# A bank of scores that one engine kept is kept half by ScalarE and half by VectorE: a gated attention mix on one core

## The chip, the cores and the metric

The kernel runs on one core of one Trainium2 chip. The metric is the device time of one execution in microseconds (us). Engines: TensorE (PE; its weight loads are PEld), VectorE (DVE), ScalarE (ACT), GpSimd (POOL) and SyncE (SP, which here issues the DMAs).

## The reference

Two attentions over the same x (2048 tokens, 448 features, 16 heads of 28) are mixed by a gate per token. A is linear attention with a learned feature map, B is full softmax attention; the change lies in B.

```python
x = A_x
g = _sigmoid((x * gate_w).sum(-1, keepdims=True))
a = _A_ref(x, A_wqkv, A_w_phi, A_wo)      # phi = softmax(p), softmax(-p) of a per-head linear map
b = _B_ref(x, B_wqkv, B_wo)
return g * a + (1 - g) * b
# _B_ref, per head:
scores = jnp.einsum("bhqd,bhkd->bhqk", q, k) * scale
p = _softmax(scores, axis=-1)
o = jnp.einsum("bhqk,bhkd->bhqd", p, v)   # then heads joined, @ wo
```

## The kernel before

Softmax needs the maximum of each query's scores over all 2048 keys before the exponentials. The kernel computes q.k twice. One pass finds the maxima: `mx_unit` does it in the first part of the run, and from about 339 us to 890 us `mx_visit` does it, beside the attention of earlier queries. The other pass (`scores`) computes the scores transposed, keys on the partitions, with the negated maximum already inside as one more row of the operands, so that ScalarE only has to take the exponential.

The main loop runs over steps s: 4 groups of 4 heads, 4 blocks of 512 queries, 16 blocks of 128 keys, so 256 steps. While maxima are left to find, a step consists of these, in this order:

- `scores(s)`: four matmuls st (L873), one for each head, each into its own bank of PSUM; ScalarE takes the exponential of each bank (L895) into p.
- `values(s - 1)`: p of the step before times v (L1004), added up in the bank pv. Each of its four matmuls shows as two.
- `mx_visit()`: the maxima for 128 queries of 4 heads against a block of 512 keys. This is the part that the change touches.

Each step with its visit is called a visit below. A block of keys has the number kb, 0 to 3. In a visit four matmuls pm (L322) go into four banks, one for each head, on different rows of the array. To halve the reductions for three of four heads, the keys kept for head j in block j are differences (`kd`, L196): max(a, b) = b + max(a - b, 0). So the bank of head kb is not reduced at once. It is read out to SBUF, through Relu where kb < 3, into the tile `rl` (L326, the kept tile; three buffers); one visit later VectorE adds it to the next bank of that head and takes the maximum of the sum (L330, two instructions: one over 512 columns, and one that reads the result). The other banks get a plain maximum each (L333). So VectorE's queue has, for kb = 1, 2, 3, two plain maxima and one sum with maximum; for kb = 0 it has three plain maxima and then the postponed maximum of the kept tile of kb = 3 (L336).

Banks of PSUM are handed out by a list, `free`, of seven; the eighth holds pv. A visit takes four. The bank that is read into `rl` is put back on the list at once, as the last one:

```python
def mx_banks(f, first):
    b = [free.pop(0) for _ in range(4)]
    free.append(b[0])
    held.extend(b[1:])
```

The next `scores` then finds four banks free: three that the exponentials have left, and fourth this one. So the fourth st matmul of a step goes into the bank that `rl` is read from in the visit before it. The other three banks of the visit come back after that `scores`, and the next visits and scores take them.

The order on each engine is written out by hand (a manual schedule); every engine takes its own queue in order. The waits between engines are put in when the program is built, from what each instruction reads and writes. At the end of a group of 16 steps VectorE copies pv out (L399), before the visit of that step; a reciprocal (L409) and a small reduction with a transposition for the maxima (L250, L255) follow in later steps.

Of the kernel before, what the change touches and what calls it, by code (L numbers as in the profile page):

```python
# [11 lines left out]
AF = mybir.ActivationFunctionType  # L12
# [28 lines left out]
def gated_mix_kernel(ctx, tc, xT, wqkB, wvB, wvA, wkAT, wqAT, phi, woA, woB,  # L41
# [7 lines left out]
    nc = tc.nc  # L49
# [136 lines left out]
    def mx_load(g, c):  # L186
        mxs[("kc", g, c)] = r = mx_tile("kc", f"kc{g}_{c}", 5)
        if c == 0:
            mxs["kd"] = mx_tile("kd", f"kd{g}", 1)
            for h in range(3):  # L190
                mx_rows(mxs["kd"], (h,), k_d[g], (h,), h * 512)
        for h in range(4):
            mx_rows(r, (h,), k_d[g], (h,), 512 * (c + (c == h and c < 3) - (c == h + 1 and c > 0)))
        if c < 3:
            js, t = slice(32 * c, 32 * c + DH), mxs["kd"]
            diffs.append((mxs["u"] + mxs["f"] // 4, lambda: nc.gpsimd.tensor_sub(  # L196
                r[js], f32(r[js]), f32(t[js]))))

    def take_diffs(n):
        while diffs and diffs[0][0] + n <= mxs["u"] + mxs["f"] // 4:  # L200
            diffs.pop(0)[1]()

    def mx_query(gq):
        g, qb = divmod(gq, NQ)
        mxs[("qc", gq)] = mx_rows(mx_tile("qc", f"qc{gq}", 3), range(4), q_d[g], range(4), qb * 512)
# [32 lines left out]
    def mx_reduce(gq):  # L238

        col = 64 * gq  # L240
        if gq < GM:
            parts = [(0, 4, col, 2)]
        elif gq == GM:
            parts = [(0, QM, col, 2), (QM, 4, col + 8 * QM, 4)]
        else:
            parts = [(0, 4, col, 4)]

        def reduce():
            for a, z, c, n in parts:
                nc.vector.tensor_reduce(  # L250
                    red[:, :16].rearrange("p (h t) -> p h t", t=4)[:, :, a:z],
                    part[:, c:c + 4 * (z - a) * n].rearrange("p (k t h) -> p h t k", t=z - a, h=4),
                    AX.X, ALU.max)
            nm_of[gq] = nm = mxp.tile([P, 32], F32, tag="nm", name=f"nm{gq}", bufs=7)
            nc.vector.transpose(nm, f32(red))  # L255

        mxs["fin"].append(reduce)
# [47 lines left out]
    def mx_visit():  # L305


        take_diffs(2)
        f = mxs["f"]
        todo = flats[f:f + 4]  # L310
        fins = mxs["fin"][:1 if todo and todo[0][1] == 0 else None]
        del mxs["fin"][:len(fins)]
        mxs["f"] = f + len(todo)
        if todo:
            gq, kb, qt, _, col = todo[0]
            g, qb = divmod(gq, NQ)
            if kb == 1 and qt in (0, QM) and gq + 1 < NG * NQ and ("qc", gq + 1) not in mxs:
                mx_query(gq + 1)
            pm = mx_banks(f, kb)
            for j in sorted(range(4), key=lambda j: j != kb):  # L320
                js = slice(32 * j, 32 * j + DH)
                nc.tensor.matmul(pm[j], mxs[("qc", gq)][js, qt * P:(qt + 1) * P],  # L322
                                 mxs[("kc", g, kb)][js, :], start=True, stop=True,
                                 tile_position=(32 * j, 0))
            rl = late_p.tile([P, 512], F32, tag="rl", name=f"rl{f}", bufs=3)
            nc.scalar.activation(rl, pm[kb], AF.Relu if kb < 3 else AF.Copy)  # L326
            for j in sorted({0, 1, 2, 3} - {kb}, key=lambda j: j == kb - 1):
                if j == kb - 1:
                    r = mxs["rl"]
                    nc.vector.tensor_tensor_reduce(r, pm[j], r, 1.0, LOWEST, ALU.add, ALU.max,  # L330
                                                   part[:, col + j:col + j + 1])
                else:
                    nc.vector.tensor_reduce(part[:, col + j:col + j + 1], pm[j], AX.X, ALU.max)  # L333
            mxs["rl"] = rl
            if kb == 3:
                mxs["fin"].append(lambda: nc.vector.tensor_reduce(  # L336
                    part[:, col + 3:col + 4], rl, AX.X, ALU.max))
            if qb == NQ - 1 and g + 1 < NG:
                if qt == 2 and kb == 3:
                    mx_load(g + 1, 0)  # L340
                if qt == 3 and kb < 3:
                    mx_load(g + 1, kb + 1)
            if qt == 3 and kb == 3:
                mx_reduce(gq)
        for fn in fins:
            fn()
# [594 lines left out]
# [4 lines that stand above are left out]
        order = [first] + sorted({0, 1, 2, 3} - {first}, key=lambda j: j == first - 1)  # L945
        return [bank(b[order.index(j)], f"pm{f}_{j}") for j in range(4)]
# [176 lines left out]
    for s in range(NS + 16):  # L1123
# [27 lines left out]
        if s:  # L1151
            mx_visit()
# [78 lines left out]
```

## Time and profile before

| what | value |
|---|---|
| median of 3 runs | 1020.08 us (1019.61 to 1020.7) |
| profiled execution | 1018.93 us |
| its span, first to last instruction | 1017.1 us |
| mean granted TensorE clock | 0.998 |
| busy: PE, DVE, ACT, POOL | 1006.6, 682.1, 817.2, 236.4 us |

The profile is of one execution. A row of a group gives line, engine, operation, output <- input with shapes and count, then busy time in us and the mean of one in ns, then the idle time of the engine just before these instructions and what ended most of it. A row of the timeline gives the start and the length in us of one instruction, or of several equal ones in a row (x2); in brackets stands how long its engine had been idle and what ended that. Matmuls are pipelined and their ends are modelled, so a PE that is busy for the whole span is not necessarily a PE that never waits; the weight loads (PEld) show better when TensorE goes on.

### The profile page before, as it was taken

The numbers are of one execution on the slowest core, as the hardware profiler recorded it, in microseconds if no ns is written. First come the engines' busy times: TensorE is split into PE (matmuls) and PEld (weight loads), VectorE is DVE, ScalarE is ACT, GpSimd is POOL, SyncE is SP. The second block draws the span as 40 slices with busy tenths as digits, with TensorE's granted clock in tenths as the row PEclk, the third lists the DMA queues.
The fourth block names the chain that finished last, engine by engine and source line by source line (L and its number), as shares of the span: only waits on it lengthen the run. The fifth ranks groups of instructions, "written<-read, shape, count | busy, mean of one in ns | idle before, by whom it ended". The sixth has DMA issues, their size and how long they took to land.

```text
span 1017.1 us, 18036 instructions
## 1 busy us (share of the span) xinstructions
PE 1006.6 (99%) x6472; PEld 563.0 (55%) x6472; DVE 682.1 (67%) x1340; ACT 817.2 (80%) x1534; POOL 236.4 (23%) x213
## 2 busy tenths in 40 slices
PE   9999999999999999999999999999999999999998
PEld 8878888878779433333333333333333333355656
DVE  5566657997753578888887888787887878710102
ACT  5445445677753899999999999999999999978682
POOL 1235456588435102110011110101201011011010
PEclk9999999999999999999999999999999999999999
DMA  8973110132345703232522223532323345516131
GB/s 298 312 236 92 58 52 1 44 90 82 91 131 122 160 14 90 58 80 69 124 68 70 55 58 78 126 68 53 87 55 75 76 100 138 144 48 163 56 111 55
DMA packets 64250, 98.89 MB, mean 97 GB/s; under 512 B 18176, under 2 KB 24944, under 8 KB 64160
## 3 DMA queue, kind: packets, MB, share of 16 engines
q1 hardware_dynamic: 64160, 97.74, 36.0%
q8 instruction: 51, 0.84, 0.3%
q14 instruction: 39, 0.32, 0.1%
HBM read 69.54 MB, written 27.78 MB: 96 GB/s over the span
## 4 chain that ended last, share of the span: by engine, by line
PE 92%; DVE 4%; DMA 1%; ACT 1%; issue 1%; SPq 0%; POOL 0%; DVEq 0%; ACTq 0%; POOLq 0%
PE st L873 29%; PE pv L1004 25%; PE pm L322 9%; PE pqk L109 5%; PE pk L127 4%; PE pva L127 4%; PE pob L109 3%; PE poa L109 3%; PE pq L109 2%; PE pvb L127 2%; PE pvb L109 1%; PE pmb L285 1%; PE pqk L652 1%; DMA dena<-oUa 1%; PE pft L525 1%; DVE fsumq L459 1%
## 5 line engine op out<-in xcount | busy, mean ns | idle before, releaser
L895 ACT ACTIVATE p<-st 128x512 f32<-128x512 f32 x1020 | 522.8, 615 | 25.6 <-PE st L873 25.5
L333 DVE TENSOR_REDUCE part<-pm 128x1 f32<-128x512 f32 x477 | 304.8, 686 | 111.1 <-PE pm L322 104.7
L873 PE MATMUL st<-qst,kst 128*128 128x512 f32 x1024 | 310.2, 427 | 0.6 <-ACT vb L715 0.5
L1004 PE MATMUL pv<-p,vb 128*32 128x512 f32 x2048 | 268.4, 604 | 0.0
L873 PEld LDWEIGHTS st<-qst,kst 128*128 128x128 f32 x1024 | 174.6, 187 | 122.3 <-issue 59.0
L322 PEld LDWEIGHTS pm<-kc,qc 28*128 28x128 f32 x848 | 40.5, 181 | 177.8 <-ACT p L895 169.4
L326 ACT ACTIVATE rl<-pm 128x512 f32<-128x512 f32 x212 | 126.9, 599 | 11.1 <-PE pm L322 0.3
L420 POOL TENSOR_TENSOR oUb<-oUb,rsb 128x512 f32<-128x512 f32 x15 | 19.4, 1291 | 464.1 <-DMA rsb<-rdb 192.6
L330 DVE CUSTOM_DVE_ANT_0 rl<-pm,rl 128x512 f32<-128x512 f32 x159 | 108.3, 681 | 0.0
L322 PE MATMUL pm<-kc,qc 28*128 28x512 f32 x848 | 107.1, 495 | 0.0
L1004 PEld LDWEIGHTS pv<-p,vb 128*32 128x32 f32 x2048 | 44.4, 108 | 70.2 <-issue 62.0
L290 DVE CUSTOM_DVE_ANT_0 rl<-pmb,rl 128x512 f32<-128x512 f32 x88 | 57.0, 686 | 29.4 <-ACT rl L288 29.4
L1016 DVE SCALAR_TENSOR_TENSOR acc<-pob,gate,acc 128x448 f32<-128x448 f32 x12 | 8.2, 684 | 90.8 <-PE pob L109 90.8
L109 PE MATMUL pqk<-XH,wB 128*128 128x512 f32 x192 | 59.3, 397 | 0.0
L288 ACT ACTIVATE rl<-pmd 128x1024 f32<-128x1024 f32 x44 | 45.2, 1028 | 12.4 <-PE pmd L285 6.0
L589 ACT CAST ev<-pqk 128x512 fp32r<-128x512 f32 x28 | 16.0, 589 | 37.3 <-PE pqk L109 32.5
L109 PE MATMUL poa<-woA_s,oTa 128*128 128x448 f32 x192 | 43.2, 374 | 0.0
L109 PEld LDWEIGHTS pqk<-XH,wB 128*128 128x128 f32 x192 | 35.4, 188 | 8.5 <-issue 1.5
L196 POOL TENSOR_TENSOR kc<-kc,kd 28x512 fp32r<-28x512 f32 x12 | 15.4, 1281 | 101.3 <-PE pm L322 60.2
L109 PE MATMUL pq<-wqA_s,XH 128*128 128x448 f32 x128 | 37.8, 378 | 0.8 <-DVE ev L590 0.8
L590 DVE TENSOR_TENSOR ev<-pqk,ev 128x512 fp32r<-128x512 f32 x28 | 19.0, 690 | 29.2 <-ACT ev L589 29.1
L109 PEld LDWEIGHTS poa<-woA_s,oTa 128*128 128x128 f32 x192 | 35.1, 188 | 5.9 <-issue 3.3
(161 smaller groups left out, 1178.0 us busy)
## 6 DMA issues: line engine op xcount, KB each, us to landing
qkd<-ev SPq DMA_DIRECT2D x28, 512.0 KB
qst<-qkd SPq DMA_DIRECT2D x64, 224.0 KB
kst<-qkd SPq DMA_DIRECT2D x64, 224.0 KB
od<-oTb SPq DMA_DIRECT2D x48, 112.0 KB
rsa<-rda SPq DMA_DIRECT2D x8, 512.0 KB
rsb<-rdb SPq DMA_DIRECT2D x15, 256.0 KB
kc<-qkd SPq DMA_DIRECT2D x64, 56.0 KB
gad<-ga SPq DMA_DIRECT2D x16, 224.0 KB
```

What stands on the lines that cost most here:

```text
L109: nc.tensor.matmul(dst, l, r, start=i == 0, stop=i == len(todo) - 1)
L127: nc.tensor.matmul(dst[:, :n], l, r, start=i == 0, stop=i == len(todo) - 1, skip_group_check=True)
L288: nc.scalar.activation(rl, pd, AF.Relu)
L290: nc.vector.tensor_tensor_reduce(rl[:, i, :], pb[:, i, :], rl[:, i, :], 1.0, LOWEST, ALU.add, ALU.max, part[:, col + i:col + i + 1])
L322: nc.tensor.matmul(pm[j], mxs[("qc", gq)][js, qt * P:(qt + 1) * P], mxs[("kc", g, kb)][js, :], start=True, stop=True, tile_position=(32 * ...
L326: nc.scalar.activation(rl, pm[kb], AF.Relu if kb < 3 else AF.Copy)
L330: nc.vector.tensor_tensor_reduce(r, pm[j], r, 1.0, LOWEST, ALU.add, ALU.max, part[:, col + j:col + j + 1])
L333: nc.vector.tensor_reduce(part[:, col + j:col + j + 1], pm[j], AX.X, ALU.max)
L420: (nc.gpsimd if n == 1 else nc.vector).tensor_mul(oU, oU, rs)
L873: nc.tensor.matmul(st, kst_of[(g, kt // 4)][:, j, (kt % 4) * P:(kt % 4 + 1) * P], qst_of[gq][:, j, :], start=True, stop=True)
L895: nc.scalar.activation(p, st, AF.Exp, scale=SCALE)
L1004: nc.tensor.matmul(pv[32 * j:32 * j + 32, :], vb[kt // 8][:, kt % 8, 4 * g + j, :], pt[j], start=kt == 0, stop=kt == NT - 1, tile_position ...
```

## The change

The kept tile gets its left 256 columns from ScalarE, and its right 256 columns from VectorE, out of the same bank: through a maximum with zero where kb < 3, as a copy where kb = 3. Nothing else is changed.

```diff
             rl = late_p.tile([P, 512], F32, tag="rl", name=f"rl{f}", bufs=3)
-            nc.scalar.activation(rl, pm[kb], AF.Relu if kb < 3 else AF.Copy)
+            nc.scalar.activation(rl[:, :256], pm[kb][:, :256], AF.Relu if kb < 3 else AF.Copy)
+            if kb < 3:
+                nc.vector.tensor_scalar_max(rl[:, 256:], pm[kb][:, 256:], 0.0)
+            else:
+                nc.vector.tensor_copy(rl[:, 256:], pm[kb][:, 256:])
```

In the built program ScalarE has as many instructions as before and VectorE has 212 more, one for each visit, ahead of that visit's maxima. The waits of one visit (kb = 0) in the changed program, with its own line numbers, are these: VectorE's half waits for ScalarE's counter, at the value which ScalarE's half of the same visit brings about, and the fourth score waits for VectorE, where it waited for ScalarE before.

```
VectorE:
L328 TensorScalarPtr rl_6213<-pm_0_6205 128x256 [waits Activation_49]
L337 TensorReduce part<-pm_1_6206 128x1 [waits PE_49]
L337 TensorReduce part<-pm_2_6207 128x1 [waits PE_49]
L337 TensorReduce part<-pm_3_6208 128x1 [waits PE_49]
L340 TensorReduce part<-rl_6179 128x1 [waits DVE_49]
TensorE:
L877 Matmult st_2_6228<-qst_3475,kst_3477 128x512 [waits DVE_49]
L877 Matmult st_3_6230<-qst_3475,kst_3477 128x512 [waits DVE_49]
```

The order on TensorE, ScalarE and GpSimd is the same as before.

## The prediction

> **What bounds the kernel now.** I read the page first, for who is busy, then the waits, then one visit in the timeline, because the shares do not say which engine holds the others.
>
> ```profile
> PE 1006.6 (99%) x6472; PEld 563.0 (55%) x6472; DVE 682.1 (67%) x1340; ACT 817.2 (80%) x1534; POOL 236.4 (23%) x213
> L333 DVE TENSOR_REDUCE part<-pm 128x1 f32<-128x512 f32 x477 | 304.8, 686 | 111.1 <-PE pm L322 104.7
> L326 ACT ACTIVATE rl<-pm 128x512 f32<-128x512 f32 x212 | 126.9, 599 | 11.1 <-PE pm L322 0.3
> ```
>
> The edited instruction is the third row: 212 reads of a 512-wide bank, 599 ns each. There is one per visit, so there are 212 visits, from the first to the last of these rows:
>
> ```profile
> 339.55 0.60 ACT L326 ACTIVATE rl<-pm 128x512 f32<-128x512 f32 x1 [0.30 <-PE pm L322]
> ...
> 889.57 0.60 ACT L326 ACTIVATE rl<-pm 128x512 f32<-128x512 f32 x1
> ```
>
> That is 550.02 us over 211 intervals, 2.607 us a visit: more than half of the run goes at the pace of this visit. Its utilisation, in one stretch of 50 us (columns PE, PEld, DVE, ACT, POOL busy, then the granted clock, DMA share, GB/s):
>
> ```profile
> 450.00:500.00 50.00, 50.00 (x309) 19.55 (x312) 40.54 (x82) 49.02 (x97) 3.19 (x3) 1.00 0.43 91
> ```
>
> ScalarE is busy 49.02 of 50, VectorE 40.54. It is tempting to stop here: ScalarE is full, VectorE has room, so half a read less on ScalarE should pay. The waits say more:
>
> ```profile
> PEld pm L322 <- ACT p L895: 169.4, 202, 0.8
> PEld st L873 <- ACT rl L326: 46.1, 212, 0.2
> ```
>
> The second row is the one that counts: in all 212 visits TensorE's weight load for a score matmul waits for this very read, 46.1 / 212 = 0.22 us each time. The first row is larger but is not a stall: the weight loader is idle for 0.84 us while TensorE streams the pv matmuls. The same 0.84 stands after the same matmuls near the end, where nothing is waited for:
>
> ```profile
> 982.86 0.56 PEld L1004 LDWEIGHTS pv<-p,vb 128*32 128x32 f32 x8 [0.30 <-issue]
> ...
> 984.26 1.11 PEld L109 LDWEIGHTS pob<-woB_s,kst 128*128 128x128 f32 x6 [0.84 <-issue]
> ```
>
> One visit, in order of time:
>
> ```profile
> 608.05 0.60 ACT L326 ACTIVATE rl<-pm 128x512 f32<-128x512 f32 x1
> 608.08 1.29 DVE L333 TENSOR_REDUCE part<-pm 128x1 f32<-128x512 f32 x2 [0.71 <-PE pm L322]
> ...
> 608.54 2.06 ACT L895 ACTIVATE p<-st 128x512 f32<-128x512 f32 x4
> 608.70 0.19 PEld L873 LDWEIGHTS st<-qst,kst 128*128 128x128 f32 x1 [0.21 <-ACT rl L326]
> 609.12 0.16 PEld L1004 LDWEIGHTS pv<-p,vb 128*32 128x32 f32 x8 [0.24 <-issue]
> ...
> 609.29 0.68 DVE L330 CUSTOM_DVE_ANT_0 rl<-pm,rl 128x512 f32<-128x512 f32 x1
> 609.89 0.08 DVE L330 DVE_READ_ACCUMULATOR2_ANT part<- 128x1 f32 x1
> 610.12 0.19 PEld L322 LDWEIGHTS pm<-kc,qc 28*128 28x128 f32 x4 [0.84 <-ACT p L895]
> ...
> 610.65 0.60 ACT L326 ACTIVATE rl<-pm 128x512 f32<-128x512 f32 x1
> ```
>
> This is a closed loop. Call T the start of the read (608.05). The read holds its bank, which the fourth score matmul needs next; that weight load starts at T+0.65 (608.70). The pv loads follow 0.42 later (609.12), the next pm loads 1.00 later (610.12), and 0.53 later the next read starts (610.65). 0.65 + 0.42 + 1.00 + 0.53 = 2.60, the whole visit. TensorE takes its work in order, so nothing can slip past the fourth score. The visit is thus set by **how long after T the bank is given back**, and only just behind that by ScalarE: four exponentials in 2.06 and the start of the read to the first of them, 0.49, make 2.55.
>
> **The change, part by part.** *ScalarE's read, halved.* The nearest row is the 256-wide copy out of a bank:
>
> ```profile
> L528 ACT COPY fT<-pft 128x256 f32<-128x256 f32 x2 | 0.8, 414 | 0.0
> L288 ACT ACTIVATE rl<-pmd 128x1024 f32<-128x1024 f32 x44 | 45.2, 1028 | 12.4 <-PE pmd L285 6.0 <-ACT z_s L489 2.4 <-ACT feat L452 1.9
> ```
>
> I take 0.414. From 1024 and 512 wide the slope is (1028 - 599) / 512 = 0.84 ns per element, which gives 599 - 214 = 385 ns as the low end; the high end is 0.44. Half the width saves a third of the time, not half.
>
> *VectorE's half, added (212 instructions).* No row before has VectorE reading 256 columns alone; the nearest are a two-operand product that reads 256 columns of a bank, and the 512-wide copy out of a bank:
>
> ```profile
> L1099 DVE TENSOR_TENSOR oUlast<-oUlast,pr 128x256 f32<-128x256 f32 x2 | 0.8, 418 | 1.3 <-PE pr L1094 1.3
> L399 DVE COPY oUb<-pv 128x512 f32<-128x512 f32 x15 | 10.4, 692 | 10.8 <-PE pv L1004 10.8
> L1090 DVE COPY rw<-rc 128x512 f32<-128x512 f32 x1 | 0.4, 426 | 0.0
> L408 DVE TENSOR_SCALAR dena<-dena 128x32 f32<-128x32 f32 x8 | 6.0, 756 | 3.1 <-DMA dena<-oUa 3.1
> 1006.74 0.75 DVE L1099 TENSOR_TENSOR oUlast<-oUlast,pr 128x256 f32<-128x256 f32 x2 [1.25 <-PE pr L1094]
> ```
>
> I take 0.42 for its duration and 0.75 - 0.42 = 0.33 for its place in the queue. Below: the copy out of SBUF (426 for 512) would scale to 0.29. Above: the dearest TENSOR_SCALAR, 0.756, although only 32 wide; it stands in a stage where POOL is busy, and POOL has 3.19 of 50 us here, so I hold that for rare.
>
> *The wait that it adds.* In the built program VectorE's half does not wait for TensorE but for ScalarE's half of the same visit, and the fourth score waits for VectorE's half. So the halves run one after the other. By the Trainium skill (PSUM — Partial Sum Buffer, section "PSUM bank collisions raise a hardware error") two engines may not read one bank in the same partitions at once, ScalarE and VectorE included, and disjoint columns do not help; by that rule the two halves have to be serial wherever they are put, which is the sum below, and without it the time would be that of the overlap rival. No trace here shows two engines in one bank at once.
>
> The two hand-overs, ScalarE to VectorE and VectorE to TensorE:
>
> ```profile
> 33.38 0.59 ACT L589 CAST ev<-pqk 128x512 fp32r<-128x512 f32 x1 [1.82 <-PE pqk L109]
> 34.00 0.69 DVE L590 TENSOR_TENSOR ev<-pqk,ev 128x512 fp32r<-128x512 f32 x1 [1.37 <-ACT ev L589]
> ...
> 1005.06 0.43 DVE L1090 COPY rw<-rc 128x512 f32<-128x512 f32 x1
> 1005.54 0.97 PEld L1094 LDWEIGHTS pr<-ident,rw 128*128 128x128 f32 x8 [0.27 <-DVE rw L1090]
> ```
>
> 34.00 - 33.97 = 0.03 and 1005.54 - 1005.49 = 0.05. The bank is given back at T + 0.414 + 0.03 + 0.42 + 0.05 = **T+0.914**, where it was T+0.65: **0.264 us later**. The other three legs (0.42, 1.00, 0.53) are TensorE's own and stay, so the visit becomes 2.607 + 0.264 = 2.87, and 212 x 0.264 = **+56 us**.
>
> *Who else stands behind the new wait.* VectorE's half is first in its queue for the visit, so the reductions behind it, which started at T+0.03, now start at T + 0.444 + 0.33 = T+0.77. They follow at 0.60 (the pair takes 1.29 with the last one at 0.69). The first two release banks for the next pm matmuls: done at T+0.77+1.29 = T+2.06, and those load from T+2.87-0.53 = T+2.34. The third frees a bank for the third score of the next visit, later still. The fullest visit (kb = 0) has three plain reductions and the postponed one on the kept tile: the queue is free at T + 0.77 + 4 x 0.60 = T+3.17, and the next half may start at T + 2.87 + 0.44 = T+3.31. It fits by 0.14. At a group's end the copy of the output bank comes ahead of the half:
>
> ```profile
> 419.97 0.69 DVE L399 COPY oUb<-pv 128x512 f32<-128x512 f32 x1 [0.28 <-PE pv L1004]
> 420.37 0.60 ACT L326 ACTIVATE rl<-pm 128x512 f32<-128x512 f32 x1
> ```
>
> It ends at 420.66, T+0.29, before the half may start: nothing. ScalarE's relief (about 0.2 a visit) is worth nothing, since it is not the last to end any more. No DMA is moved; those that VectorE's results release have a longer visit to land in. Before 339 us and after 890 us nothing changes.
>
> **Sum.** The profiled execution took 1018.93 for a span of 1017.1; the span becomes 1073, that execution 1075. The median of the runs shown is 1020.08, 1.15 higher: **1076 us**.
>
> **Rivals.** *The halves overlap, faster.* If VectorE read its columns while ScalarE reads its own, the bank would come back at T + 0.42 + 0.05 = T+0.47, 0.18 earlier, and 212 x 0.18 = 38 gives 982 us; ScalarE's own 2.06 + 0.3 would allow that. It decides when VectorE starts before T+0.18, from which on the leg is under 0.65. For it: VectorE waits idle for the pm matmuls, 0.71 us in the row at 608.08. Against it: the wait on ScalarE's half, by which VectorE cannot start before T+0.44. 4%.
>
> *Nothing changes*, 1020, if the fourth score were not on the path. The 212 waits of 0.22 us and the sum 2.60 speak against it. 2%.
>
> *VectorE is dearer or late.* If its half takes 0.45 to 0.50, that is 6 to 17 us more; if POOL's work stretches it to 0.756 in a tenth of the visits, 21 x 0.34 = 7 more; and past the 0.14 of room each kb = 0 visit (53 of them) pays, 5 us for each 0.1. Together 1082 to 1094. For it: VectorE's half becomes a link of the loop, so every delay in its queue reaches TensorE. 16%.
>
> *The clock falls.* The stall in front of the fourth score grows from 0.22 to 0.48 of a visit. The mean clock was below 1.00 in one stretch, and there the trace has a gap of TensorE behind VectorE:
>
> ```profile
> 200.00:300.00 100.00, 96.62 (x711) 75.40 (x709) 76.13 (x152) 73.74 (x117) 65.87 (x49) 0.98 0.31 93
> 213.61 0.50 PE L285 MATMUL pmd<-kp,qp 28*128 28x512 f32 x2 [2.12 <-DVE part L290]
> ```
>
> At half clock TensorE's legs, 1.95 together, could at most double: a tenth of the visits so would cost 21 x 1.95 = 41 us, 1117. Against it: the gaps of 0.22 left the clock at 1.00, and 0.48 is far below the 2.12 of that row. 4%. The Trainium skill (TensorE: Matmul & The Clock Gate, "A second HAM failure mode: psum-queue depth-cycling") tells of a kernel whose frequent short idles between groups of matmuls made the clock fall and rise again; the row at 450 us, with a short idle in each visit and a clock of 1.00, does not show it.
>
> **How the numbers follow.** The forecast, serial halves at about these prices, has 74% and the time 1076. The cheapest ends, 0.385 and 0.35, would give 0.165 a visit, 1055, and VectorE's 0.29 still less; I trust the 418-ns row more and put the low end at 1060, where the leg is 0.19 longer. The high end takes in the late VectorE: 1094. About 0.2% (2 us) is what a measurement of this kernel can tell from no change. Faster 4%, same 2%, slower 94%.
>
> **What would show it.** Right: the wait of the fourth score is put down to VectorE's new instruction, 212 times, about 0.48 us each (102 us in all); reads start 2.87 us apart; VectorE's half starts 0.44 after ScalarE's; ScalarE's busy time in a 50-us stretch falls to about 43; the clock stays 1.00. Wrong: halves that overlap, a VectorE half far from 0.42, a visit that grows by other than the later bank, or a wait of the pm matmuls for reductions.

## The result and the profile after

| | before | after |
|---|---|---|
| median of 6 runs | 1019.33 us (1018.41 to 1020.7) | 1072.69 us (1070.4 to 1075.67) |
| profiled execution: time, span | 1018.93, 1017.1 us | 1075.67, 1073.9 us |

The changed kernel takes 1.0519 times as long (95% interval 1.0506 to 1.0532), 53.4 us more by the medians. The forecast was 56 more, 1076 us.

The page after: the busy times; then the read that is now halved, with VectorE's two new forms (through a maximum, as a copy), and the weight loads of the scores. After the bar stands the idle time of the engine before these instructions and what ended it.

```profile
PE 1054.2 (98%) x6472; PEld 563.6 (52%) x6472; DVE 751.7 (70%) x1552; ACT 794.2 (74%) x1534; POOL 235.3 (22%) x213
...
L877 PEld LDWEIGHTS st<-qst,kst 128*128 128x128 f32 x1024 | 174.6, 187 | 175.1 <-DVE rl L328 74.0
L326 ACT ACTIVATE rl<-pm 128x256 f32<-128x256 f32 x212 | 81.5, 384 | 74.7 <-PE pm L322 74.7
...
L328 DVE TENSOR_SCALAR rl<-pm 128x256 f32<-128x256 f32 x159 | 67.5, 424 | 75.4 <-ACT rl L326 72.8
...
L330 DVE COPY rl<-pm 128x256 f32<-128x256 f32 x53 | 22.5, 424 | 23.2 <-ACT rl L326 22.8
```

ScalarE's read fell from 599 to 384 ns, and ScalarE now waits 0.35 us in each visit for pm (74.7 / 212), where it had been idle for 0.05 (11.1 / 212 in the row before). VectorE's halves take 424 ns. Who waits for them, from the views of their two lines:

```profile
who waited for it (us, times):
  PEld st L877: 74.0, 159
...
  PEld st L877: 24.6, 53
```

Together 212 waits of the fourth score and 98.6 us, where before there were 46.1. One visit after, in order of time:

```profile
600.20 0.38 ACT L326 ACTIVATE rl<-pm 128x256 f32<-128x256 f32 x1 [0.35 <-PE pm L322]
600.62 0.42 DVE L328 TENSOR_SCALAR rl<-pm 128x256 f32<-128x256 f32 x1 [0.63 <-ACT rl L326]
600.64 2.06 ACT L899 ACTIVATE p<-st 128x512 f32<-128x512 f32 x4
600.96 1.28 DVE L337 TENSOR_REDUCE part<-pm 128x1 f32<-128x512 f32 x2
601.10 0.19 PEld L877 LDWEIGHTS st<-qst,kst 128*128 128x128 f32 x1 [0.46 <-DVE rl L328]
601.52 0.16 PEld L1008 LDWEIGHTS pv<-p,vb 128*32 128x32 f32 x8 [0.24 <-issue]
...
602.52 0.19 PEld L322 LDWEIGHTS pm<-kc,qc 28*128 28x128 f32 x4 [0.84 <-ACT p L899]
...
603.05 0.38 ACT L326 ACTIVATE rl<-pm 128x256 f32<-128x256 f32 x1 [0.34 <-PE pm L322]
```

From the read to the fourth score's load: 601.10 - 600.20 = 0.90 us (0.65 before). Then 0.42, 1.00 and 0.53, as before. VectorE sits idle for 0.63 us until ScalarE's half is done, and only then begins; in all 212 visits of this trace its half starts 0.415 to 0.418 us after ScalarE's.

The length of a visit comes from the first and the last read, 211 visits apart (view of line 326 after: min/median/max in ns, then first and last start):

```profile
L326 ACT ACTIVATE rl<-pm x212: 383/385/386, 343.1 to 945.5; 128x256 f32<-128x256 f32 x106
```

(945.5 - 343.1) / 211 = 2.855 us, 0.248 more than before. So 52.4 of the 56.8 us by which the span grew lie in these visits. The first read comes 3.6 us later than before (343.1 against 339.55 us), behind a part of the program that the change does not touch. In the executions below it comes anywhere from 337.4 to 341.4 us, and the profiled execution is the slowest of the six, 3.0 us above their median; so this is put down to the execution, not to the change. It has a gap of TensorE of 1.73 us at 227 us, which the execution before does not have. The other 0.8 lies behind the last read.

### The profile page after: what moved, and what is told of

It is laid out like the page before. It is cut to its first block, busy times and chain, and to the rows that moved or that the text cites. A ratio compares the mean times of both kernels' runs of the same rounds, so it can differ in the third digit from the quotient of the medians.

```text
span 1073.9 us, 18193 instructions
## 1 busy us (share of the span) xinstructions
PE 1054.2 (98%) x6472; PEld 563.6 (52%) x6472; DVE 751.7 (70%) x1552; ACT 794.2 (74%) x1534; POOL 235.3 (22%) x213
## 4 chain that ended last, share of the span: by engine, by line
PE 91%; DMA 4%; DVE 2%; issue 1%; ACT 1%; POOL 0%; SPq 0%; POOLq 0%; ACTq 0%
PE st L877 31%; PE pv L1008 23%; PE pm L322 9%; PE pqk L109 4%; PE pk L127 4%; PE pva L127 3%; PE pob L109 3%; PE poa L109 3%; PE pq L109 3%; PE pvb L127 2%; DMA dena<-oUa 2%; PE pvb L109 1%; PE pmb L285 1%; PE pft L529 1%; PE pqk L656 1%; DMA rsa<-rda 1%
## 5 line engine op out<-in xcount | busy, mean ns | idle before, releaser
L877 PE MATMUL st<-qst,kst 128*128 128x512 f32 x1024 | 356.7, 439 | 7.3 <-ACT vb L719 0.5
L326 ACT ACTIVATE rl<-pm 128x256 f32<-128x256 f32 x212 | 81.5, 384 | 74.7 <-PE pm L322 74.7
L328 DVE TENSOR_SCALAR rl<-pm 128x256 f32<-128x256 f32 x159 | 67.5, 424 | 75.4 <-ACT rl L326 72.8
L330 DVE COPY rl<-pm 128x256 f32<-128x256 f32 x53 | 22.5, 424 | 23.2 <-ACT rl L326 22.8
```

What stands on the lines that cost most here:

```text
L326: nc.scalar.activation(rl[:, :256], pm[kb][:, :256], AF.Relu if kb < 3 else AF.Copy)
L328: nc.vector.tensor_scalar_max(rl[:, 256:], pm[kb][:, 256:], 0.0)
L877: nc.tensor.matmul(st, kst_of[(g, kt // 4)][:, j, (kt % 4) * P:(kt % 4 + 1) * P], qst_of[gq][:, j, :], start=True, stop=True)
```

## The experiments

The theory: the two reads of the bank are serial, the fourth score waits for the second, and that wait is the whole cost. The rivals: VectorE's 212 instructions, or the later reductions behind them, cost by themselves; or the kept tile, not the bank, makes the halves serial. The last column is taken from the first and the last read, 211 visits apart, as above.

| kernel | median us | ratio to before (95%) | us a visit |
|---|---|---|---|
| VectorE's half from another bank | 1009.44 | 0.9918 (0.9898 to 0.9938) | 2.561 |
| 480 columns and 32 | 1062.69 | 1.0429 (1.0414 to 1.0445) | 2.809 |
| VectorE alone | 1059.34 | 1.0399 (1.0382 to 1.0416) | 2.798 |
| halves by rows | 1172.78 | 1.1513 (1.1486 to 1.1541) | 3.332 |
| before, two pv matmuls ahead | 1255.12 | 1.2322 (1.2301 to 1.2342) | 3.722 |
| split, two pv matmuls ahead | 1256.36 | 1.2331 (1.2313 to 1.2349) | 3.722 |
| before, four pv matmuls ahead | 1067.79 | 1.0486 (1.047 to 1.0501) | 2.840 |
| split, four pv matmuls ahead | 1067.5 | 1.048 (1.0464 to 1.0496) | 2.840 |

**Another bank.** The halves stay, but VectorE reads the right half from a bank that ScalarE does not touch:

```diff
+            other = pm[0 if kb else 1]
...
-                nc.vector.tensor_scalar_max(rl[:, 256:], pm[kb][:, 256:], 0.0)
+                nc.vector.tensor_scalar_max(rl[:, 256:], other[:, 256:], 0.0)
...
-                nc.vector.tensor_copy(rl[:, 256:], pm[kb][:, 256:])
+                nc.vector.tensor_copy(rl[:, 256:], other[:, 256:])
```

> Left out: the right half of the kept tile is read from another bank of the same visit (the one that VectorE reduces first), so the values kept there are not the maxima of this head. Same tile, same number of instructions, same widths, but the two engines no longer read one bank, and VectorE's half waits for TensorE instead of ScalarE. My theory (the halves are serial because they share the bank): the bank comes back 0.385 + 0.05 = 0.435 us after the read starts instead of 0.90, TensorE's loop falls to 2.607 - 0.215 = 2.39, and ScalarE with 0.44 to its first exponential and 2.06 for the four becomes the bound at 2.50 us a visit; 212 x 0.107 = 23 us below before, about 997 us. Rival (they are serial because they write one kept tile, or VectorE's 212 instructions cost by themselves): as the changed kernel, about 1072 us, and the fourth score still waits about 0.46 us.

1009.44 us: a little faster than before, by under 1% but clear of the noise. (For kb = 1 the other bank is not the one that VectorE reduces first but the one that it adds last; the widths and the instructions are the same.) One visit:

```profile
602.33 0.19 PEld L322 LDWEIGHTS pm<-kc,qc 28*128 28x128 f32 x4 [0.84 <-ACT p L900]
...
602.76 0.77 PEld L878 LDWEIGHTS st<-qst,kst 128*128 128x128 f32 x4 [0.24 <-issue]
...
602.87 0.39 ACT L326 ACTIVATE rl<-pm 128x256 f32<-128x256 f32 x1
602.90 0.42 DVE L331 COPY rl<-pm 128x256 f32<-128x256 f32 x1 [0.22 <-PE pm L322]
...
603.89 0.16 PEld L1009 LDWEIGHTS pv<-p,vb 128*32 128x32 f32 x8 [0.36 <-issue]
...
604.89 0.19 PEld L322 LDWEIGHTS pm<-kc,qc 28*128 28x128 f32 x4 [0.84 <-ACT p L900]
```

The two reads start 0.03 us apart in this visit and run side by side; the four scores load in one row with no wait. The kept tile is the same and the instructions as many, so neither makes the halves serial nor costs 53 us: sharing the bank does, through the wait that the built program puts between the two reads. What the engines would do with one bank without that wait, no run shows. The size was missed: 997 was expected. With no wait left, TensorE's own groups fill the visit: 0.43 from the pm load to the scores, 1.13 to the pv loads, 1.00 to the next pm, 2.56 us. Before, in the visit that the prediction shows, the scores begin here:

```profile
607.95 0.54 PEld L873 LDWEIGHTS st<-qst,kst 128*128 128x128 f32 x3 [0.24 <-issue]
```

To the pv loads at 609.12 they took 1.17, with a stall of 0.21 among them. Without it they take 1.13: the four loads in one row take 0.77, not 0.54 + 0.19 = 0.73, and the pv loads follow 0.36 after the last of them, not 0.24. Most of that stall was not there to be won.

**A sliver.** Edit: 480 in place of each 256, so that VectorE reads 32 columns.

> ScalarE reads 480 columns and VectorE the last 32. My theory (two reads one after the other, each with a fixed part): ScalarE 0.385 + 0.214 x 224/256 = 0.572, VectorE 0.424 - 0.235 = 0.19, hand-overs 0.08, bank back at 0.84 us, 0.19 later than before: 212 x 0.19 = 41 us, about 1060 us. Rival (the cost goes with the columns that VectorE takes): 32/256 of 53 us, about 1026 us.

1062.69 us, a visit of 2.809, 0.202 more than before. The reads:

```profile
604.74 0.57 ACT L326 ACTIVATE rl<-pm 128x480 f32<-128x480 f32 x1 [0.28 <-PE pm L322]
605.21 2.06 ACT L899 ACTIVATE p<-st 128x512 f32<-128x512 f32 x4
605.35 0.19 DVE L328 TENSOR_SCALAR rl<-pm 128x32 f32<-128x32 f32 x1 [0.81 <-ACT rl L326]
605.46 1.28 DVE L337 TENSOR_REDUCE part<-pm 128x1 f32<-128x512 f32 x2
605.59 0.19 PEld L877 LDWEIGHTS st<-qst,kst 128*128 128x128 f32 x1 [0.42 <-DVE rl L328]
```

The bank is back after 605.59 - 604.74 = 0.85 us. Handing 32 of 512 columns to VectorE costs four fifths of handing over half: the two reads together take 0.57 + 0.19 = 0.76 us here, 0.38 + 0.42 = 0.81 with halves and 0.60 as one. It is the second read's fixed part and the hand-over that are paid, hardly the columns.

**VectorE alone.** The three lines that keep the tile become `tensor_scalar_max(rl, pm[kb], 0.0)` or `tensor_copy(rl, pm[kb])`, and ScalarE's read goes.

> VectorE keeps the whole bank, ScalarE nothing. One read, no hand-over between engines: about 0.03 + 0.69 + 0.05 = 0.77 us until the bank is back, 0.12 later than before: 212 x 0.12 = 25 us, about 1045 us, if only the bank's return counts. My theory adds VectorE's queue, which now has work for 5 x 0.605 = 3.03 us in the visits with kb = 0, longer than the visit of 2.73: there TensorE has to wait for VectorE to come to its read, 53 x 0.30 = 16 us more, about 1061 us. Rival (two reads are no worse than one, the changed kernel loses by VectorE's added load): slower than the changed kernel, above 1073 us.

1059.34 us, against 1061 expected. One read by the slower engine beats two shared reads, as the bank comes back earlier (702.75 to 703.49, 0.74):

```profile
702.75 0.69 DVE L327 TENSOR_SCALAR rl<-pm 128x512 f32<-128x512 f32 x1 [0.22 <-PE pm L322]
...
703.49 0.19 PEld L876 LDWEIGHTS st<-qst,kst 128*128 128x128 f32 x1 [0.32 <-DVE rl L327]
...
708.15 0.69 DVE L327 TENSOR_SCALAR rl<-pm 128x512 f32<-128x512 f32 x1 [0.20 <-PE pm L322]
...
708.76 1.88 DVE L336 TENSOR_REDUCE part<-pm 128x1 f32<-128x512 f32 x3
...
710.55 0.68 DVE L339 TENSOR_REDUCE part<-rl 128x1 f32<-128x512 f32 x1
...
711.14 0.68 DVE L327 TENSOR_SCALAR rl<-pm 128x512 f32<-128x512 f32 x1
...
711.88 0.19 PEld L876 LDWEIGHTS st<-qst,kst 128*128 128x128 f32 x1 [0.59 <-DVE rl L327]
```

Here the late VectorE of the prediction is seen: from a read with kb = 0 to the next is 711.14 - 708.15 = 2.99 us, all of it VectorE's own work with no idle time in brackets, where the read at 702.75 was followed by one at 705.45, 2.70 later. That 1061 was met so closely is in part luck: the leg is 0.03 us shorter than expected, and 25 more visits are late that the expectation left out, 13 behind the copy of pv (3.01 us) and 12 behind the small reduction (2.83).

**By rows.** ScalarE gets `rl[:64]` and VectorE `rl[64:]`, all 512 columns each.

> The bank is divided by partitions: ScalarE reads rows 0 to 63 and VectorE rows 64 to 127, all 512 columns each. In the built program VectorE still waits for ScalarE. My theory: a read's time goes by its columns, so neither gets shorter, and the bank is back after 0.60 + 0.03 + 0.69 + 0.05 = 1.37 us, 0.72 later than before: 212 x 0.72 = 153 us, about 1172 us. Rival (the time goes by elements): half rows cost what half columns cost, about 1073 us.

1172.78 us, from two runs. Half the rows save nothing: the reads take 592 and 694 ns.

```profile
701.10 0.59 ACT L326 ACTIVATE rl<-pm 64x512 f32<-64x512 f32 x1 [0.81 <-PE pm L322]
701.59 2.03 ACT L899 ACTIVATE p<-st 128x512 f32<-128x512 f32 x4
701.72 0.69 DVE L328 TENSOR_SCALAR rl<-pm 64x512 f32<-64x512 f32 x1 [0.71 <-ACT rl L326]
702.45 1.89 DVE L337 TENSOR_REDUCE part<-pm 128x1 f32<-128x512 f32 x3
702.47 0.19 PEld L877 LDWEIGHTS st<-qst,kst 128*128 128x128 f32 x1 [0.94 <-DVE rl L328]
```

The bank is back after 1.37 us and the visit is 3.332. Over before, the four legs with one rule (0.65, 0.85, 0.90, 1.37) give 0, 0.202, 0.248 and 0.725 us a visit: the visit grows by what the leg grows, to within 0.01.

**Two pv matmuls ahead of the fourth score**, in the kernel before and in the changed one. The core of the edit, which takes the wait off the path by moving the fourth score behind other work:

```diff
         for j in (2 * i, 2 * i + 1):
+            if mid and j == 3:
+                mid()
             used.append(free.pop(0))
...
                     scores(z, 0)
-                    scores(z, 1)
+                    scores(z, 1, (lambda: values(s - 1, (0, 1))) if s < TWO else None)
...
-            values(s - 1)
+            values(s - 1, (2, 3) if s < TWO else range(4))
```

> The kernel before, with one thing moved: two of the four pv matmuls of the step stand ahead of the fourth score on TensorE. My theory (the fourth score stalls TensorE 0.22 us in each visit, and this is on the path): the two pv matmuls take 0.5 us and cover it, TensorE's loop becomes 2.39, and ScalarE's 0.49 + 2.06 = 2.55 is next: 212 x 0.05 = 11 us faster, about 1009 us. Rival (the stall is hidden, ScalarE alone sets the pace): no change, 1020 us.

> The changed kernel with the same two pv matmuls ahead of the fourth score, which then is wanted 0.44 + 0.50 = 0.94 us after the read starts, when the bank is back (0.90). My theory (the whole loss of the change is this wait): the loss goes, and ScalarE's shorter read counts for the first time: 0.44 + 2.06 = 2.50 us a visit, 212 x 0.107 = 23 us below before, about 997 us. Rival (VectorE's queue becomes late in the visits with four reductions, since it is free at 3.17 us and wanted at 2.94): 53 x 0.2 = 10 us more, about 1007 us. Second rival (VectorE's 212 instructions cost by themselves): above 1050 us.

1255.12 and 1256.36 us: both expectations fail by some 250 us, for one reason above all. The loads of one visit (before, two ahead):

```profile
701.18 0.19 PEld L322 LDWEIGHTS pm<-kc,qc 28*128 28x128 f32 x4 [0.84 <-ACT p L897]
...
701.61 0.53 PEld L873 LDWEIGHTS st<-qst,kst 128*128 128x128 f32 x3 [0.24 <-issue]
...
702.51 0.14 PEld L1006 LDWEIGHTS pv<-p,vb 128*32 128x32 f32 x4 [0.36 <-issue]
...
703.49 0.19 PEld L873 LDWEIGHTS st<-qst,kst 128*128 128x128 f32 x1 [0.84 <-ACT p L897]
...
703.92 0.14 PEld L1006 LDWEIGHTS pv<-p,vb 128*32 128x32 f32 x4 [0.25 <-issue]
...
704.91 0.19 PEld L322 LDWEIGHTS pm<-kc,qc 28*128 28x128 f32 x4 [0.84 <-ACT p L897]
```

Two pv matmuls take TensorE 0.98 us, and four took 1.00: the four lie on different columns of the array, and by these times they run together. Cutting the group in two pays for it twice, and TensorE's groups sum to 0.43 + 0.90 + 0.98 + 0.43 + 0.99 = 3.73 us. But as a pair the two kernels answer the question: with the fourth score out of the bank's way, the split kernel and the one before both have a visit of 3.722 us. The change's 53 us are gone, though in a visit so long that much else could hide in it; the next pair has a shorter one.

**Four pv matmuls ahead**, the same with the group whole (`mid` is `values(s - 1)`).

> The kernel before with all four pv matmuls ahead of the fourth score, not two. From the trace of the version with two ahead, TensorE's groups take 0.43 (pm), 0.90 (three scores), 0.98 (pv, be it two or four) and 0.43 (the fourth score): 2.74 us a visit, 0.13 more than before: 212 x 0.13 = 28 us, about 1048 us, and no wait for the kept tile's bank. Rival (the order of the groups is free and only the stall goes): 2.56 us a visit as with the other bank, about 1010 us.

> The changed kernel with the same order, all four pv matmuls ahead of the fourth score, which is then wanted about 1.4 us after the read starts, while the bank is back at 0.90. My theory (the change costs only through the wait of the fourth score): the same as its partner without the split, about 1048 us, and 25 us faster than the changed kernel. Rival (VectorE's 212 instructions or its later reductions cost as well): slower than its partner by more than 5 us.

1067.79 and 1067.5 us, a visit of 2.840 in both. The pair is equal again, as expected: in a visit of this length VectorE's 212 instructions and the later reductions cost nothing. The level was missed by 20 us: in this order three scores take 0.98 to the pv loads, not 0.90, and pv 1.00, so the groups sum to 0.44 + 0.98 + 1.00 + 0.42 = 2.84 (version before: loads of pm at 702.28 us, three scores 702.72, pv 703.70, the fourth score 704.70, pm 705.12). This order loses more by TensorE's groups than the stall was worth. Apart from the version with another bank, which keeps other values, none of these kernels is faster than the one before.

## Why the prediction was right, and where it was not

- **The loop.** Right. The three legs that were to stay did (0.42, 1.00, 0.53), and the first went from 0.65 to 0.90 with a forecast of 0.914. The pairs with the moved fourth score show no other cost.
- **ScalarE's half.** Taken as 0.414 from a copy, it was 0.384; the low end, from the slope between 512 and 1024 columns, hit it (385 ns). Those 0.03 us x 212 = 6 us are more than the whole miss of the sum; the hand-overs, together 0.01 longer, give some of it back.
- **VectorE's half.** 0.42 forecast, 0.424 measured, never above 0.425; the dear end of 0.756 did not come.
- **The wait.** It is put down to VectorE's instruction in all 212 visits, 0.47 us each (0.48 forecast); VectorE starts 0.42 after ScalarE (0.44 forecast). That two reads of one bank are put one after the other is what the Trainium skill (PSUM — Partial Sum Buffer, "PSUM bank collisions raise a hardware error") asks for. In this kernel the built program does it with a wait: VectorE idles for 0.63 us in the visit shown, and with another bank the two reads start 0.03 us apart. No run has two engines in one bank at once, so what would happen then is not shown here.
- **Room on VectorE.** It was enough, no pm load waits for a reduction, before or after. In a visit with kb = 0 the read starts at 605.91 us; the queue was to be free at T+3.17 and the next half to start at T+3.31:

```profile
608.46 0.67 DVE L340 TENSOR_REDUCE part<-rl 128x1 f32<-128x512 f32 x1
...
609.19 0.42 DVE L328 TENSOR_SCALAR rl<-pm 128x256 f32<-128x256 f32 x1
```

  The last reduction ends at T+3.22 and the half starts at T+3.28, so VectorE goes on almost without a break and is still in time. The copy at a group's end, which was to be over at T+0.29, comes behind the sum of the visit before and ends later than forecast, but still before the half may start:

```profile
614.18 0.69 DVE L403 COPY oUb<-pv 128x512 f32<-128x512 f32 x1
...
614.48 0.38 ACT L326 ACTIVATE rl<-pm 128x256 f32<-128x256 f32 x1 [0.35 <-PE pm L322]
...
614.90 0.42 DVE L330 COPY rl<-pm 128x256 f32<-128x256 f32 x1
```

  It ends at T+0.39 and the half starts at T+0.42: right by 0.03 us, with less room than the prediction saw.
- **ScalarE's relief is worth nothing.** Right: 43.02 of 50 us busy from 450 to 500 us (about 43 forecast), and the time rose.
- **The clock.** The stretch from 450 to 500 us has a clock of 1.00 after, too; the rival did not come. From 200 to 300 us, where the prediction set a clock of 0.98 beside a gap of TensorE, it is 1.00 in this execution, although nearly the same gap is there and TensorE is no busier. So a gap of 2 us need not lower the clock.

```profile
216.42 0.50 PE L285 MATMUL pmd<-kp,qp 28*128 28x512 f32 x2 [2.09 <-DVE part L290]
...
200.00:300.00 100.00, 95.09 (x710) 74.44 (x708) 77.41 (x152) 74.08 (x120) 64.17 (x48) 1.00 0.30 88
...
450.00:500.00 50.00, 49.44 (x285) 17.70 (x284) 43.14 (x94) 43.02 (x88) 7.38 (x8) 1.00 0.29 67
```

- **The price of the overlap rival was wrong.** 982 us left out TensorE's own floor: with the reads side by side the run takes 1009. The prediction read the stall of 0.22 us as TensorE's to win; 0.046 of it was (2.607 - 2.561). Nor would the exponentials have allowed 982: the first of them starts 0.44 us after the read (600.64 - 600.20 in the visit after), not 0.3, and 0.44 + 2.06 = 2.50 is more than the 2.43 that 982 needs.
- **The sum of the rival in which VectorE is dearer or late was wrong.** Its terms, 6 to 17, 7 and 5 us for each 0.1, reach 1100 us and more, not 1094. None of the three came, so the range held all the same.

## What to carry to other kernels

Before an eviction is shared by two engines, look for what the bank's return releases: in every version here in which both read the same bank, the program let one read wait for the other, so the parts added up, each with its fixed cost, and the sliver shows that even 32 columns cost 0.20 us a visit. Utilisation said that ScalarE was full and VectorE had room; the wait of one weight load, 212 times, said what the time hung on. A stall in front of an engine is an upper bound of what taking it away can win, and the engine's other groups have to be added up first.

## What had not been expected of the hardware

Four pv matmuls on different columns of the array cost TensorE 1.00 us and two of them 0.98. A read of a bank was not shortened by taking half the rows: ScalarE took 592 ns for 64 rows of 512 columns, and for 128 rows 598 in the median before and 592 with four pv matmuls ahead; VectorE took 694 for 64 rows and 691 for 128 (medians). The pv loads come 0.24 us after a fourth score that had just stalled, and 0.36 after scores that load in one row. With the 0.04 that the four loads take longer in one row, that leaves 0.05 of a stall of 0.21.
